# Scores as three float16 products with scaled queries and keys, from the eighteenth tile on, in an attention and channel-mix kernel

## The chip, the cores and the metric

The kernel runs on one core of a Trainium2 chip. The metric is the device time of one launch in microseconds. A core has five engines that each work through their own list of instructions in order: PE multiplies matrices (PEld, its weight load, overlaps it), DVE and POOL do elementwise work and reductions, ACT evaluates functions and scaled copies, and SP issues the DMA transfers. The engines wait for one another through semaphores.

## The reference

An attention without heads over pooled keys is followed by a channel mix. B is 4, there are N = 12288 queries of C = 128 channels per batch, and the keys and values are the same 768 vectors per batch.

```python
kv_pool = kv.reshape(B, H // r, r, W // r, r, C).mean(axis=(2, 4))     # r = 4
k = v = kv_pool.reshape(B, -1, C) @ w_sr                               # 768 x 128
s = (q @ k.transpose(0, 2, 1)) / sqrt(C)
a = exp(s - s.max(-1)); a /= a.sum(-1) + 1e-09
x = a @ v
xk = mu_k * x + (1.0 - mu_k) * x_prev        # x_prev: the row before, zero at the start
xr = mu_r * x + (1.0 - mu_r) * x_prev
kk = np.maximum(xk @ w_k, 0.0)               # 128 -> 1024
out = sigmoid(xr @ w_r) * (kk * kk @ w_v)    # 1024 -> 128
```

The inputs make the scores and the gates large, so every product of matrices is carried to more than one half-precision factor.

## The kernel before

The work is cut into tiles of 512 queries, 24 per batch; the last one is cut in two of 256, so there are 97 tiles. One tile goes through these steps. Their short names are the keys of the tables that set the order.

- `qf` loads the queries (channels on partitions), `qh` (ACT) rounds them to float32r, `ql` (POOL) is the rest in bfloat16.
- `S0` to `S3` (PE): scores of 128 queries against 768 keys, in a PSUM buffer of two banks. Each is three products in two chunks of columns (256 and 512): `ql` with the keys in bfloat16, the upper half of `qh` read as bfloat16 with the rest of the keys (`kbl` holds both), and `qh` with the keys in float32r (`ksh`).
- `nm` (DVE): the row maximum, negated. `ex` (ACT): exponential with `nm` as bias and the row sum as a second output. `rc` (DVE): the reciprocal of the sums. `f1` (ACT) and `f2` (DVE): the weights in float16 and their rest. `tt` (SP): the DMA transposes into `pT`.
- `AV0` to `AV5` (PE): 18 products of 512 columns into `px`. `xe`, `xc`, `x`, `xh`, `xl` on ACT, POOL and DVE: the mix with the row before, split in two float16 halves.
- `ha`, `hb` 0 to 3 (PE): the first layer, two blocks of 128 each, 24 products. `r`, `k2`, `kh`, `kl`: relu and square on ACT and DVE, the split on ACT, DVE and POOL. `va`, `vb` (PE): the second layer, 24 products. `z` (PE): the gate, 3 products; `th`, `E`, `T1`, `E1`, `g` finish it; `o` multiplies, `so` stores.

Each group of instructions is added to a plan with a number as its time: the entry of its name in a table plus the tile's place times PERIOD (19.3). All groups of all tiles are issued in the order of these numbers, and each engine gets its instructions in that order. The tables are ONCE (weights and first batch), EARLY (the first 8 tiles), WHEN (the tiles between), LATE (the last 5), PREP and SUM (the keys of the next batch). SUM adds one load and one reduction of 64 keys (`L`, `br`) to each of 12 tiles of each of the first three batches; PREP adds the projection (`pk`), scale statistics (`am` to `xt`, `sv`) and the splits of the keys (`ksh`, `kb`, `kd`, and `vh`, `vl`, `tv` for the values).

PSUM holds three buffers of two banks in a ring named "big", which the four scores and the four blocks of the first layer of each tile take in turn, and one bank each named "x" (`px`, `pz`, and the small products of the preparation) and "v" (`pv`). A product can be issued only once the buffer's last user has been read. Three of the four exponentials are written to SBUF; that of `S3` stays in PSUM until `f2`. Of the four blocks of the first layer, `k2` of block 3 is written over the product in PSUM, and DVE makes its `kl` from there.

In the profile nearly all instructions carry line 39, the helper that records them. So groups are told apart by the tiles that they write and read.

Of the kernel before, what the change touches and what calls it, by code (L numbers as in the profile page):

```python
# [73 lines left out]
def tile_kernel(ctx, tc, qT, kv0a, kv0b, kvw, head, w_k, w_v, w_r, outT):  # L74
# [16 lines left out]
    scale = 1.0 / math.sqrt(C)  # L91

# [26 lines left out]
    for name, shape, dtype in (  # L119
# [11 lines left out]
        ("ks", [P, K], F32), ("acc", [P, K], F32), ("dg", [P, 2, P], BF16), ("di", [P, P], F32),  # L131
# [319 lines left out]
    def batch_prep(b, i0, res):  # L451
# [18 lines left out]
        ex, exs, ivs = (one(n) for n in ("ex", "exs", "ivs"))  # L470
        xt, xi = (one(n, n=2) for n in ("xt", "xi"))
        exi = one("exi", I32)

        for n, (c0, c1) in enumerate(CHUNKS):
            @at(f"ksh{n}")
            def _(n=n, c0=c0, c1=c1):
                if later:
                    dve.tensor_copy(out=put("ksh")[:, c0:c1], in_=ks[:, c0:c1])
                else:
                    act.activation(  # L480
                        out=put("ksh")[:, c0:c1], in_=pks[n][:, 0:c1 - c0], func=AF.Copy,
                        scale=scale / WIN,
                    )

            @at(f"kb{n}")
            def _(n=n, c0=c0, c1=c1):
                if later:
                    pool.tensor_copy(out=put("kbl")[:, 0, c0:c1], in_=ks[:, c0:c1])
                else:
                    act.activation(  # L490
                        out=put("kbl")[:, 0, c0:c1], in_=pks[n][:, 0:c1 - c0], func=AF.Copy,
                        scale=scale / WIN,
                    )

            @at(f"kd{n}")
            def _(n=n, c0=c0, c1=c1):
                if later:
                    pool.tensor_tensor(
                        out=put("kbl")[:, 1, c0:c1], in0=ks[:, c0:c1],
                        in1=res["ksh"][:, c0:c1].bitcast(F32), op=ALU.subtract,  # L500
                    )
                else:
                    dve.scalar_tensor_tensor(
                        out=put("kbl")[:, 1, c0:c1], in0=pks[n][:, 0:c1 - c0], scalar=scale / WIN,
                        in1=res["ksh"][:, c0:c1].bitcast(F32), op0=ALU.mult, op1=ALU.subtract,
                    )
# [74 lines left out]
    def plan_tile(i, b, t0, T, at0):  # L581
# [36 lines left out]

        @at("qh")
        def _():  # L620
            act.copy(out=new("qh"), in_=st["qf"])

        @at("ql")
        def _():
            pool.tensor_tensor(
                out=new("ql"), in0=st["qf"], in1=st["qh"].bitcast(F32), op=ALU.subtract
            )

        for s in range(NSUB):
# [18 lines left out]

            @at(f"ex{s}")
            def _(s=s):  # L650
# [4 lines left out]
                else:  # L655
# [3 lines left out]
                    bias=st[f"nm{s}"], scale=1.0, accum_out=st[f"sm{group[s]}"][:, s:s + 1],  # L659
# [238 lines left out]
    bps = {b: {} for b in range(B)}  # L898

# [19 lines left out]
BUFS = {'pe': 4, 'nm': 4, 'sm': 4, 'rc': 4, 'pp': 4, 'kk': 3, 'kh': 4, 'kl': 4, 'kv': 6, 'rr': 2, 'ks': 1, 'acc': 1, 'dg': 1, 'vv': 1, 'di': 2}  # L919
FIRST = [512]  # L920
LAST = [256, 256]
ENGINE = {'wq': 'P', 'wp': 'P', 'wd': 'P', 'cz': 'P', 'cv': 'P', 'uz': 'P', 'vl': 'P', 'am': 'D'}
BLOCKS = [2, 2, 2, 2, 2, 2, 2, 2]
GROUP = 8

WHEN = {
# [7 lines left out]
    "xck": 141.87398, "xek": 142.03537, "xer": 142.22498, "xk": 142.40427, "xr": 142.58396,  # L934
# [19 lines left out]
    "L": 65.37223, "br": 79.195,  # L954
# [339 lines left out]
```

## Time and profile before

| what | value |
|---|---|
| median of 3 runs | 1876.15 us (1875.62 to 1876.49) |
| profiled execution, its own time | 1878.05 us |
| its span in the trace | 1876.3 us |
| PE, PEld busy | 1842.5 us (98%), 932.4 us (50%) |
| DVE, ACT, POOL busy | 1711.5 us (91%), 1698.2 us (91%), 1061.1 us (57%) |
| mean granted clock of PE | 0.996 |
| DMA queue of SP, share of 16 engines | 59.6%, 230.43 MB |

Busy time is the time in which at least one instruction of the engine runs. Two instructions of an engine that follow each other overlap at their ends, so busy times of single instructions add up to more than the engine's. The ends of products on PE are modelled; their starts are not, so the distance from one start to the next is the better measure there.

### The profile page before, as it was taken

The page shows a single profiled execution, that of the slowest core. Times are in us where ns is not written, and L with a number is a line of the kernel's source. Part 1 is how long each engine was busy: PE and PEld are TensorE (multiplying, and loading weights), DVE is VectorE, ACT ScalarE, POOL GpSimd, SP SyncE. Part 2 cuts the span into 40 slices and gives each one's busy share as a digit, 9 for nine tenths or more (in the row PEclk, how much of TensorE's full clock was granted, in tenths as well). Part 3 has the DMA queues.
Part 4 walks back from the last instruction along what each step waited for, and adds up shares of the span by engine and source line. Part 5 has one row for each costly group of instructions (what it writes and reads, how often), then busy time and mean ns, then how long its engine had stood idle before and what let it go on. Part 6 is the DMA issues. An engine that isn't in the chain of part 4 may idle for free.

```text
span 1876.3 us, 26840 instructions
## 1 busy us (share of the span) xinstructions
PE 1842.5 (98%) x8918; PEld 932.4 (50%) x9065; DVE 1711.5 (91%) x2383; ACT 1698.2 (91%) x2454; POOL 1061.1 (57%) x818
## 2 busy tenths in 40 slices
PE   6999999999999999999999999999999999999999
PEld 3444455454545455555555454545455555555545
DVE  6899999999899999999989999999998989898898
ACT  5998999999999999999999999989999999999987
POOL 3555655565555555556555565656555555555556
PEclk8999999999999999999999999999999999999999
DMA  7766566565657675656555666747465556555462
GB/s 230 141 136 143 124 151 117 112 122 108 117 124 146 135 144 138 115 110 119 113 112 129 146 134 143 139 101 131 102 119 107 115 110 116 110 111 109 92 118 61
DMA packets 644235, 232.15 MB, mean 124 GB/s; under 512 B 612352, under 2 KB 613120, under 8 KB 644096
## 3 DMA queue, kind: packets, MB, share of 16 engines
q1 hardware_dynamic: 644096, 230.43, 59.6%
q8 instruction: 71, 1.16, 0.3%
q14 instruction: 68, 0.56, 0.1%
HBM read 52.63 MB, written 25.17 MB: 41 GB/s over the span
## 4 chain that ended last, share of the span: by engine, by line
PE 91%; DVE 1%; issue 1%; DMA 0%; ACT 0%; SPq 0%; DVEq 0%; ACTq 0%
PE ph L39 25%; PE pv L39 25%; PE px L39 19%; PE S L39 19%; PE pz L39 4%; DMA pT<-pp 0%; PE pk L39 0%; DVE pp L39 0%; DVE nm L39 0%; DVE kk L39 0%; DVE xr L39 0%; ACT kh L39 0%; DVE xk L39 0%; ACT xer L39 0%; DVE kl L39 0%
## 5 line engine op out<-in xcount | busy, mean ns | idle before, releaser
L39 POOL TENSOR_TENSOR kl<-kk,kh 128x1024 bf16<-128x1024 f32 (+1 forms) x291 | 663.7, 2281 | 238.1 <-ACT kh L39 186.1
L39 ACT ACTIVATE rr<-ph 128x1024 f32<-128x1024 f32 (+1 forms) x388 | 393.2, 1015 | 59.0 <-PE ph L39 46.6
L39 DVE TENSOR_REDUCE nm<-S 128x1 f32<-128x768 f32 x384 | 364.9, 952 | 69.8 <-PE S L39 69.5
L39 PE MATMUL px<-pT,vT 128*128 128x512 f16 (+1 forms) x1746 | 393.1, 378 | 0.9 <-DMA pT<-pp 0.6
L39 ACT ACTIVATE kh<-rr 128x1024 f16<-128x1024 f32 (+1 forms) x291 | 305.0, 1049 | 1.3 <-PE pv L39 0.8
L39 DVE SCALAR_TENSOR_TENSOR pp<-pe,rc,pp 128x768 f16<-128x768 f32 x289 | 293.6, 1018 | 2.6 <-ACT pp L39 2.4
L39 PE MATMUL pv<-kh,wvl 128*128 128x512 f16 (+1 forms) x776 | 294.7, 381 | 0.0
L39 PE MATMUL ph<-xkh,wkl 128*128 128x512 f16 (+1 forms) x776 | 292.2, 377 | 0.7 <-ACT pe L39 0.3
L39 PE MATMUL ph<-xkh,wkh 128*128 128x512 f16 (+1 forms) x776 | 292.2, 377 | 0.0
L39 PE MATMUL pv<-kh,wvh 128*128 128x512 f16 (+1 forms) x776 | 292.1, 377 | 0.0
L39 PEld LDWEIGHTS <-vT 128*128 128x128 f16 x1746 | 170.4, 98 | 205.3 <-issue 2.4
L39 PE MATMUL S<-ksh,qh 128*128 128x512 f32 (+1 forms) x768 | 270.7, 434 | 0.0
L39 ACT ACTIVATE pp<-pe,rc 128x768 f16<-128x768 f32 x289 | 267.9, 931 | 1.0 <-DMA pT<-pp 0.9
L39 ACT ACTIVATE pe<-S,nm 128x768 f32<-128x768 f32 x289 | 260.1, 900 | 6.8 <-DVE nm L39 6.6
L39 POOL TENSOR_TENSOR xrl<-xr,xrh 128x512 f16<-128x512 f32 (+1 forms) x97 | 112.1, 1155 | 271.9 <-DVE xrh L39 271.9
L39 PE MATMUL S<-kbl,qh 128*128 128x256 bf16 (+1 forms) x768 | 252.7, 329 | 3.0 <-issue 0.2
L39 POOL TENSOR_TENSOR xkl<-xk,xkh 128x512 f16<-128x512 f32 (+1 forms) x97 | 114.7, 1182 | 243.7 <-DVE xkh L39 237.5
L39 DVE TENSOR_TENSOR kk<-ph,rr 128x1024 f32<-128x1024 f32 (+1 forms) x194 | 233.9, 1206 | 15.9 <-ACT rr L39 15.9
L39 PEld LDWEIGHTS <-wkh 128*128 128x128 f16 x1552 | 151.4, 98 | 179.4 <-issue 2.8
L39 PE MATMUL ph<-xkl,wkh 128*128 128x512 f16 (+1 forms) x776 | 228.8, 377 | 0.1
L39 PE MATMUL S<-kbl,ql 128*128 128x512 bf16 (+1 forms) x714 | 215.0, 326 | 5.8 <-DVE pp L39 3.0
L39 PE MATMUL pv<-kl,wvb 128*128 128x512 bf16 (+1 forms) x683 | 201.1, 377 | 2.6
(118 smaller groups left out, 2628.2 us busy)
## 6 DMA issues: line engine op xcount, KB each, us to landing
qf<-qT SPq DMA_DIRECT2D x95, 256.0 KB, 3.0
outT<-o SPq DMA_DIRECT2D x95, 256.0 KB, 3.3
kvt<-kvw SPq DMA_DIRECT2D x36, 512.0 KB, 4.7
pT<-pp SPq DMA_TRANSPOSE x384, 3.9
kva<-kv0a SPq DMA_DIRECT2D x8, 512.0 KB, 8.2
kvb<-kv0b SPq DMA_DIRECT2D x4, 512.0 KB, 5.8
land<-moe_w_k SPq DMA_DIRECT2D x2, 512.0 KB, 6.1
land<-moe_w_v SPq DMA_DIRECT2D x2, 512.0 KB, 7.3
```

Of the source, the lines that this page charges most:

```text
L39: return self.tc.keep_in_program_order(op(*args, **kwargs))
```

## The change

Tiles 0 to 16 keep the scores described above. From tile 17 on (`half`), the queries of eight tiles (a turn; `GROUP`) share one scale, and the keys of a batch another:

- `Lq` loads a tile's queries a second time, nine tiles ahead (`AHEAD`), and `mq` (ACT) takes the sum of their absolute values per channel, with an accumulated output. At the last tile of a turn, `qr` (DVE) takes the largest of the eight, `qd` (ACT) puts it on a diagonal, `qb` (PE) multiplies by ones so that every partition has all 128 values, `qt` (DVE) takes the largest, and `qg` (DVE) makes the scale and its inverse. The sum bounds the largest value from above.
- `qs` (POOL) multiplies the loaded queries by the inverse scale in place; `qh` and `ql` are float16 then.
- A third diagonal block (`dg`, `dm`, `xt` have three columns now) gives the largest key of a batch; `kfh` (ACT) and `kfl` (DVE) make the keys' two float16 parts in `kf`. They take the place of `ksh`, `kb` and `kd` for the second to fourth batch, whose keys no longer have them; the first batch has both.
- `S` is `ql` with the upper keys, `qh` with the lower, `qh` with the upper, all float16.
- `gs` (DVE) is the product of the two scales per turn and batch; `nm` is followed by a multiplication by it (DVE, one column), and `ex` has it as its scale operand.

The numbers of all tables are new as well, so the order of the whole program differs. PERIOD, the ring sizes (but for one of the new tiles) and the split of the other work over the engines are the same. WHEN has 93 entries where it had 84.

```diff
+    AHEAD = GROUP + 1
+    half_from = START
...
-        for n, (c0, c1) in enumerate(CHUNKS):
+        for n, (c0, c1) in enumerate(CHUNKS if not later else []):
             @at(f"ksh{n}")
...
+            dve.tensor_scalar_mul(st["dg"][:, 2, :], ident, ex)
...
         @at("sv")
         def _():
             dve.reciprocal(xi, xt)
+            dve.tensor_scalar_mul(sk, xi[:, 2:3], X_TOP)
+            dve.tensor_copy(out=put("bk"), in_=xt[:, 2:3])
...
+        @at("kfh")
+        def _():
+            act.activation(out=put("kf")[:, 0, :], in_=ks, func=AF.Copy, scale=sk)
+
+        @at("kfl")
+        def _():
+            dve.scalar_tensor_tensor(
+                out=put("kf")[:, 1, :], in0=ks, scalar=sk, in1=put("kf")[:, 0, :],
+                op0=ALU.mult, op1=ALU.subtract,
+            )
...
+        half = i >= half_from
+        turn, place = divmod(i - half_from, GROUP)
+
+        if half_from <= i + AHEAD < NTILES:
+            b2, t2, T2, _at2 = seq[i + AHEAD]
+            turn2, place2 = divmod(i + AHEAD - half_from, GROUP)
+            ends = place2 == GROUP - 1 or i + AHEAD == NTILES - 1
+            gq = groups.setdefault(turn2, {})
+
+            @at("Lq")
+            def _():
+                st["qm"] = take("qm")
+                sp.dma_start(out=st["qm"][:, 0:T2], in_=qT[b2, :, t2:t2 + T2])
+
+            @at("mq")
+            def _():
...
+                if ENGINE["mq"] == "A":
+                    act.activation(
+                        out=take("ju")[:, 0:T2], in_=st["qm"][:, 0:T2], func=AF.Abs,
+                        accum_out=gq["mq"][:, place2:place2 + 1],
+                    )
...
+            if ends:
+                @at("qr")
+                def _():
+                    dve.tensor_reduce(
+                        out=one("qr"), in_=gq["mq"][:, 0:place2 + 1], axis=AX.X, op=ALU.max
+                    )
+
+                @at("qd")
+                def _():
+                    gq["dq"] = take("dq")
+                    act.activation(out=gq["dq"], in_=ident, func=AF.Copy, scale=one("qr"))
+
+                @at("qb")
+                def _():
+                    gq["pq"] = take("x", name="pq")[:, 0:P]
+                    pe.matmul(gq["pq"], lhsT=ones, rhs=gq["dq"], start=True, stop=True)
+
+                @at("qt")
+                def _():
+                    dve.tensor_reduce(out=one("qt"), in_=gq["pq"], axis=AX.X, op=ALU.max)
+
+                @at("qg")
+                def _():
+                    gq["bq"], gq["sq"] = take("bq"), take("sq")
+                    dve.tensor_scalar(
+                        gq["bq"], one("qt"), 2.0 ** -90, 1.0 / X_TOP, op0=ALU.max, op1=ALU.mult
+                    )
+                    dve.reciprocal(gq["sq"], gq["bq"])
...
+        if half:
+            @at("qs")
+            def _():
+                eng("qs").tensor_scalar_mul(st["qf"], st["qf"], groups[turn]["sq"])
...
+                if half:
+                    kf = bps[b]["kf"]
+                    for c0, c1 in CHUNKS[::-1]:
+                        for m, (w, h) in enumerate(((ql, 0), (qh, 1), (qh, 0))):
+                            pe.matmul(
+                                S[:, c0:c1], lhsT=w, rhs=kf[:, h, c0:c1], start=(m == 0), stop=(m == 2)
+                            )
+                    return
...
+                if half:
+                    st["gs"] = units[turn, b]
+                    dve.tensor_scalar_mul(st[f"nm{s}"], st[f"nm{s}"], st["gs"])
...
-                    bias=st[f"nm{s}"], scale=1.0, accum_out=st[f"sm{group[s]}"][:, s:s + 1],
+                    bias=st[f"nm{s}"], scale=st["gs"] if half else 1.0, accum_out=st[f"sm{group[s]}"][:, s:s + 1],
...
+START = 17
...
-    "qf": 58.22684, "qh": 90.77762, "ql": 96.17481, "S0": 103.60711, "S1": 103.79064,
+    "qf": 59.2816, "Lq": 60, "mq": 80, "qs": 86, "qh": 90.45951, "qr": 93.6, "ql": 93.65377,
+    "qd": 93.8, "qb": 94.2, "qt": 94.6, "qg": 95, "S0": 105.76747, "S1": 106.49731,
```

The first place is PE at one score in the middle of the program. Names ahead of the arrow are what is written, names behind it what is read. Before, it is:

```order
L39 LDWEIGHTS ql
L39 MATMUL S<-kbl,ql 128x256
L39 LDWEIGHTS qh
L39 MATMUL S<-kbl,qh 128x256
L39 LDWEIGHTS ql
L39 MATMUL S<-kbl,ql 128x512
L39 LDWEIGHTS qh
L39 MATMUL S<-kbl,qh 128x512
L39 MATMUL S<-ksh,qh 128x512
L39 MATMUL S<-ksh,qh 128x256
```

Now the same place reads:

```order
L39 LDWEIGHTS ql
L39 MATMUL S<-kf,ql 128x256
L39 LDWEIGHTS qh
L39 MATMUL S<-kf,qh 128x256
L39 LDWEIGHTS qh
L39 MATMUL S<-kf,qh 128x256
L39 LDWEIGHTS ql
L39 MATMUL S<-kf,ql 128x512
L39 LDWEIGHTS qh
L39 MATMUL S<-kf,qh 128x512
L39 LDWEIGHTS qh
L39 MATMUL S<-kf,qh 128x512
```

The two float32r products, whose weight loads are not instructions of their own here, are gone, and all six products have a weight load of the same kind.

The second place is DVE between the last two row maxima of a tile and the next block of the gate. Before:

```order
L39 TENSOR_TENSOR ph<-ph,rr 128x1024
L39 TENSOR_REDUCE nm<-S 128x1
L39 TENSOR_TENSOR kl<-ph,kh 128x1024
L39 TENSOR_REDUCE nm<-S 128x1
L39 TENSOR_SCALAR E<-E,sc 128x512
L39 TENSOR_SCALAR th<-th 128x512
L39 SCALAR_TENSOR_TENSOR E<-th,E 128x512
L39 TENSOR_SCALAR rc<-sm 128x4
L39 RECIPROCAL rc<-rc 128x4
```

Now, in a tile that ends a turn of eight:

```order
L39 TENSOR_TENSOR ph<-ph,rr 128x1024
L39 TENSOR_REDUCE nm<-S 128x1
L39 TENSOR_SCALAR nm<-nm,gs 128x1
L39 TENSOR_TENSOR kl<-ph,kh 128x1024
L39 TENSOR_REDUCE nm<-S 128x1
L39 TENSOR_SCALAR nm<-nm,gs 128x1
L39 TENSOR_REDUCE qr<-mq 128x1
L39 TENSOR_REDUCE qt<-pq 128x1
L39 TENSOR_SCALAR bq<-qt 128x1
L39 RECIPROCAL sq<-bq 128x1
L39 TENSOR_SCALAR E<-E,sc 128x512
L39 TENSOR_SCALAR th<-th 128x512
```

Each row maximum has its multiplication right behind it, and in one tile of eight the four small instructions of the turn stand ahead of the gate and of `rc`.

The third place is ACT from the gate of one tile to the first relu of the next. Before:

```order
L39 ACTIVATE E<-pz,uz 128x512
L39 ACTIVATE th<-pz,uz 128x512
L39 ACTIVATE pe,sm<-S,nm 128x768
L39 ACTIVATE S,sm<-S,nm 128x768
L39 ACTIVATE rr<-ph 128x1024
```

Now, in a tile that ends a turn:

```order
L39 CAST qh<-qf 128x512
L39 ACTIVATE th<-pz,uz 128x512
L39 ACTIVATE E<-pz,uz 128x512
L39 ACTIVATE pe,sm<-S,nm,gs 128x768
L39 ACTIVATE dq<-ident,qr 128x128
L39 ACTIVATE S,sm<-S,nm,gs 128x768
L39 ACTIVATE ju,mq<-qm 128x512
L39 ACTIVATE rr<-ph 128x1024
```

The exponentials read `gs` besides `nm`, the pass over the second copy of the queries stands between the last exponential and the first relu, and in one tile of eight `dq` stands between the two exponentials.

More of the change, by code (lines that the diff above doesn't have):

```diff
@@ L130, in tile_kernel @@
         ("s4", [P, 4], F32), ("uz", [P, 2], F32), ("sc", [P, 1], F32),
-        ("ks", [P, K], F32), ("acc", [P, K], F32), ("dg", [P, 2, P], BF16), ("di", [P, P], F32),
+        ("ks", [P, K], F32), ("acc", [P, K], F32), ("dg", [P, 3, P], BF16), ("di", [P, P], F32), ("kf", [P, 2, K], F16), ("qm", [P, T], F32), ("mq", [P, GROUP], F32), ("ju", [P, T], BF16),
+        ("bk", [P, 1], F32), ("bq", [P, 1], F32), ("sq", [P, 1], F32), ("gs", [P, 1], F32), ("dq", [P, P], BF16),
     ):
@@ L469, in batch_prep @@
         pks = later_keys(b, i0, at, ks) if later else first_keys(ks)
-        ex, exs, ivs = (one(n) for n in ("ex", "exs", "ivs"))
-        xt, xi = (one(n, n=2) for n in ("xt", "xi"))
+        ex, exs, ivs, sk = (one(n) for n in ("ex", "exs", "ivs", "sk"))
+        xt, xi = (one(n, n=3) for n in ("xt", "xi"))
         exi = one("exi", I32)
-        for n, (c0, c1) in enumerate(CHUNKS):
+        for n, (c0, c1) in enumerate(CHUNKS if not later else []):
             @at(f"ksh{n}")
             def _(n=n, c0=c0, c1=c1):
[L477 to L483, printed above, removed]
+                act.activation(
+                    out=put("ksh")[:, c0:c1], in_=pks[n][:, 0:c1 - c0], func=AF.Copy, scale=scale / WIN
+                )
@@ L485, in _ @@
             @at(f"kb{n}")
             def _(n=n, c0=c0, c1=c1):
[L487 to L493, printed above, removed]
+                act.activation(
+                    out=put("kbl")[:, 0, c0:c1], in_=pks[n][:, 0:c1 - c0], func=AF.Copy,
+                    scale=scale / WIN,
+                )
@@ L495, in _ @@
             @at(f"kd{n}")
             def _(n=n, c0=c0, c1=c1):
[L497 to L506, printed above, removed]
+                dve.scalar_tensor_tensor(
+                    out=put("kbl")[:, 1, c0:c1], in0=pks[n][:, 0:c1 - c0], scalar=scale / WIN,
+                    in1=res["ksh"][:, c0:c1].bitcast(F32), op0=ALU.mult, op1=ALU.subtract,
+                )
@@ L556, in _ @@
                 )
+            dve.tensor_scalar_mul(st["dg"][:, 2, :], ident, ex)
         @at("dm")
         def _():
-            st["dm"] = take("x", name="dm", shape=[P, 2, P])
+            st["dm"] = take("x", name="dm", shape=[P, 3, P])
             pe.matmul(st["dm"], lhsT=ones, rhs=st["dg"], start=True, stop=True)
@@ L574, in _ @@
                 )
+        @at("kfh")
[3 more added lines that the diff above has]
+        def _():
+            dve.scalar_tensor_tensor(
+                out=put("kf")[:, 1, :], in0=ks, scalar=sk, in1=put("kf")[:, 0, :],
+                op0=ALU.mult, op1=ALU.subtract,
+            )
         @at("uz")
@@ L617, in _ @@
             sp.dma_start(out=new("qf"), in_=qT[b, :, t0:t0 + T])
+        half = i >= half_from
[11 more added lines that the diff above has]
+            def _():
+                if "mq" not in gq:
+                    gq["mq"] = take("mq")
+                if ENGINE["mq"] == "A":
+                    act.activation(
+                        out=take("ju")[:, 0:T2], in_=st["qm"][:, 0:T2], func=AF.Abs,
+                        accum_out=gq["mq"][:, place2:place2 + 1],
+                    )
+                else:
+                    dve.tensor_reduce(
+                        out=gq["mq"][:, place2:place2 + 1], in_=st["qm"][:, 0:T2], axis=AX.X,
+                        op=ALU.max, apply_absolute_value=True,
+                    )
+            if ends:
+                @at("qr")
+                def _():
+                    dve.tensor_reduce(
+                        out=one("qr"), in_=gq["mq"][:, 0:place2 + 1], axis=AX.X, op=ALU.max
+                    )
+                @at("qd")
[14 more added lines that the diff above has]
+                        gq["bq"], one("qt"), 2.0 ** -90, 1.0 / X_TOP, op0=ALU.max, op1=ALU.mult
+                    )
+                    dve.reciprocal(gq["sq"], gq["bq"])
@@ L619, in _ @@
+        if half and (place == 0 or t0 == 0 or i == half_from):
+            @at("gs")
+            def _():
+                units[turn, b] = take("gs")
+                dve.tensor_scalar(
+                    units[turn, b], groups[turn]["bq"], bps[b]["bk"], 1.0 / X_TOP, op0=ALU.mult,
+                    op1=ALU.mult,
+                )
+        if half:
+            @at("qs")
+            def _():
+                eng("qs").tensor_scalar_mul(st["qf"], st["qf"], groups[turn]["sq"])
         @at("qh")
@@ L620, in _ @@
         def _():
-            act.copy(out=new("qh"), in_=st["qf"])
+            if half:
+                st["qh"] = take("qh", shape=[P, TOP], dtype=F16)[:, 0:T]
+            else:
+                new("qh")
+            act.copy(out=st["qh"], in_=st["qf"])
         @at("ql")
         def _():
+            if half:
+                st["ql"] = take("ql", dtype=F16)[:, 0:T]
+            else:
+                new("ql")
             pool.tensor_tensor(
-                out=new("ql"), in0=st["qf"], in1=st["qh"].bitcast(F32), op=ALU.subtract
+                out=st["ql"], in0=st["qf"], in1=st["qh"] if half else st["qh"].bitcast(F32),
+                op=ALU.subtract,
@@ L631, in _ @@
             def _(s=s):
-                ksh, kbl = bps[b]["ksh"], bps[b]["kbl"]
                 S = st[f"S{s}"] = take("big", name="S")
@@ L635, in _ @@
                 qh, ql = st["qh"][:, sl], st["ql"][:, sl]
+                if half:
+                    kf = bps[b]["kf"]
[3 more added lines that the diff above has]
+                                S[:, c0:c1], lhsT=w, rhs=kf[:, h, c0:c1], start=(m == 0), stop=(m == 2)
+                            )
+                    return
+                ksh, kbl = bps[b]["ksh"], bps[b]["kbl"]
                 qb = st["qh"].bitcast(BF16).rearrange("p (t h) -> p t h", h=2)[:, sl, 1]
@@ L647, in _ @@
                 )
+                if half:
+                    st["gs"] = units[turn, b]
+                    dve.tensor_scalar_mul(st[f"nm{s}"], st[f"nm{s}"], st["gs"])
             @at(f"ex{s}")
@@ L898, in tile_kernel @@
     bps = {b: {} for b in range(B)}
+    groups, units = {}, {}
     batch_prep(0, 0, bps[0])
@@ L918 @@
 PAIRS = 8
-BUFS = {'pe': 4, 'nm': 4, 'sm': 4, 'rc': 4, 'pp': 4, 'kk': 3, 'kh': 4, 'kl': 4, 'kv': 6, 'rr': 2, 'ks': 1, 'acc': 1, 'dg': 1, 'vv': 1, 'di': 2}
+BUFS = {'pe': 4, 'nm': 4, 'sm': 4, 'rc': 4, 'pp': 4, 'kk': 3, 'kh': 4, 'kl': 4, 'kv': 6, 'rr': 2, 'ks': 1, 'acc': 1, 'dg': 1, 'vv': 1, 'di': 2, 'ju': 1}
 FIRST = [512]
 LAST = [256, 256]
-ENGINE = {'wq': 'P', 'wp': 'P', 'wd': 'P', 'cz': 'P', 'cv': 'P', 'uz': 'P', 'vl': 'P', 'am': 'D'}
+ENGINE = {'wq': 'P', 'wp': 'P', 'wd': 'P', 'cz': 'P', 'cv': 'P', 'uz': 'P', 'vl': 'P', 'am': 'D', 'mq': 'A', 'qs': 'P'}
 BLOCKS = [2, 2, 2, 2, 2, 2, 2, 2]
 GROUP = 8
+START = 17
 WHEN = {
[7 rows of a table removed]
-    "xck": 141.87398, "xek": 142.03537, "xer": 142.22498, "xk": 142.40427, "xr": 142.58396,
[9 rows of a table removed]
[8 rows of a table added]
+    "AV2": 143.76038, "xcr": 144.20781, "xek": 144.74705, "xer": 145.91357, "xk": 146.12634,
[9 rows of a table added]
 }
 PREP = {
[4 rows of a table removed]
[3 rows of a table added]
 }
 SUM = {
-    "L": 65.37223, "br": 79.195,
+    "L": 60.34821, "br": 75.22001,
 }
 ONCE = {
[30 rows of a table removed]
[28 rows of a table added]
+    "kfl": 213.51421,
 }
@@ L1146 @@
     {
[17 rows of a table removed]
-    },
-    {
[7 rows of a table removed]
-        "xck": 142.94987, "xek": 144.24683, "xk": 145.03802, "xer": 145.9814, "xr": 146.10995,
[9 rows of a table removed]
-    },
-    {
[7 rows of a table removed]
-        "AV4": 142.50543, "xek": 143.55947, "xk": 144.17765, "xkh": 144.80629, "xer": 146.00366,
[9 rows of a table removed]
-    },
-    {
[5 rows of a table removed]
-        "xek": 138.09887, "xk": 142.47605, "xr": 142.53025, "xkh": 143.84478, "xkl": 147.51737,
[9 rows of a table removed]
-    },
-    {
[5 rows of a table removed]
-        "xck": 148.36922, "xk": 148.39723, "xr": 149.91817, "xkh": 150.7783, "xkl": 152.61305,
[9 rows of a table removed]
[7 rows of a table added]
+        "xcr": 142.18496, "xck": 142.18855, "xer": 143.40538, "xek": 143.56156, "xr": 143.85997,
+        "xk": 144.31728, "xkh": 151.18973, "xrh": 152.30643, "xkl": 154.54183, "ha0": 154.67368,
[8 rows of a table added]
+    },
+    {
[7 rows of a table added]
+        "AV1": 141.58135, "xcr": 142.34413, "xek": 143.8, "xer": 145.993, "xk": 146.17206,
[9 rows of a table added]
+    },
+    {
[17 rows of a table added]
+    },
+    {
[5 rows of a table added]
+        "xek": 142.20235, "xk": 142.37284, "xkh": 144.92548, "xkl": 145.19568, "xer": 145.25123,
[9 rows of a table added]
+    },
+    {
[5 rows of a table added]
+        "xer": 154.07119, "xek": 154.27859, "xr": 154.34528, "xrh": 155.56082, "xrl": 157.34039,
[9 rows of a table added]
     },
```

11 lines of the change are left out of this document (3 added, 8 removed), and 509 rows, old and new, of tables (EARLY, LATE, ONCE, PREP).

## The prediction

> **What bounds the kernel now.** I read the page's busy shares and its chain of waits first, then the chain in order of time, then PE's instructions around one score, then the busy time by stretch, and last the groups of instructions of ACT, DVE and POOL.
>
> ```profile
> span 1876.3 us, 26840 instructions
> PE 1842.5 (98%) x8918; PEld 932.4 (50%) x9065; DVE 1711.5 (91%) x2383; ACT 1698.2 (91%) x2454; POOL 1061.1 (57%) x818
> PE 91%; DVE 1%; issue 1%; DMA 0%; ACT 0%; SPq 0%; DVEq 0%; ACTq 0%
> ```
>
> PE alone makes up 91% of the chain. In order of time (start, length, what), the chain shows the same piece again and again, the 18 products of `px`:
>
> ```profile
> 749.32 3.88 PE px L39 x18
> 769.79 3.88 PE px L39 x18
> ...
> 978.26 3.88 PE px L39 x18
> 997.20 3.88 PE px L39 x18
> 1016.14 3.88 PE px L39 x18
> ```
>
> From one to the next are 18.94 us, to the hundredth, tile after tile. Where the keys of a batch are prepared it is 20.47 once (749.32 to 769.79), for PE has its own products to add there. One product of 512 columns takes 3.88 / 18 = 0.2156 us. A tile has 18 + 24 + 24 + 3 = 69 of them outside the scores, 14.87 us. The four scores get the rest, 18.94 - 14.87 = 4.07 us, or 1.017 each. So the tile is PE's list without gaps, and only what shortens this list, or puts a gap in it, moves the time.
>
> PE's instructions around one score (start, length, engine, operation):
>
> ```profile
> 1010.65 0.27 PE L39 MATMUL S<-kbl,ql 128*128 128x256 bf16 x1
> 1010.75 0.27 PE L39 MATMUL S<-kbl,qh 128*128 128x256 bf16 x1
> 1010.86 0.38 PE L39 MATMUL S<-kbl,ql 128*128 128x512 bf16 x1
> 1011.08 0.38 PE L39 MATMUL S<-kbl,qh 128*128 128x512 bf16 x1
> 1011.11 0.70 PE L39 MATMUL S<-ksh,qh 128*128 128x512 f32 x2
> 1011.65 0.39 PE L39 MATMUL pv<-kh,wvl 128*128 128x512 f16 x1
> ```
>
> By the starts a score takes 1.00 us up to the next product; the tile's sum gives 1.017, the difference being a slower first product behind it.
>
> **The change part by part.** *The products.* The number of columns stays the same: three times 768. The float32r pair was already nearly as fast as half precision, so this is not a change from slow to fast products. The trace has chains of 256-column float16 products with a weight load each, in the last tile:
>
> ```profile
> 1859.74 0.27 PE L39 MATMUL ph<-xkh,wkh 128*128 128x256 f16 x1
> 1859.84 0.27 PE L39 MATMUL ph<-xkh,wkl 128*128 128x256 f16 x1
> 1859.95 0.27 PE L39 MATMUL ph<-xkh,wkh 128*128 128x256 f16 x1
> 1860.06 0.38 PE L39 MATMUL ph<-xkl,wkh 128*128 128x256 f16 x2
> ```
>
> Their starts are 0.32 / 3 = 0.107 apart. A float16 score is then 3 x (0.2156 + 0.107) = 0.968 us. Against 1.00 it saves 0.03, against 1.017 it saves 0.049; four scores save 0.12 to 0.20 us per tile. The tile's sum is measured end to end, so I lean to its side and take 0.165. Tiles 17 to 96 are 78 whole and two half ones, 79 in all: 13.0 us (bounds 9.5 to 15.8). A tile then has 18.94 - 0.165 = 18.775 us for every other engine.
>
> *ACT and DVE must fit into that.* Busy time in one tile without and one with a reduction of the next batch's keys, and at both ends of the program (start:end, length, then each engine):
>
> ```profile
> core 0: us, PE busy (x) PEld busy (x) DVE busy (x) ACT busy (x) POOL busy (x), PEclk, DMA share, GB/s
> 420.00:438.94 18.94, 18.89 (x94) 9.51 (x93) 17.03 (x27) 17.42 (x26) 10.31 (x9) 1.00 0.57 99
> 610.00:628.94 18.94, 18.89 (x94) 9.53 (x94) 17.97 (x25) 17.42 (x26) 11.02 (x9) 1.00 0.65 139
> ...
> 0.00:52.00 52.00, 33.23 (x110) 17.40 (x113) 36.50 (x82) 28.63 (x53) 20.05 (x26) 0.89 0.75 229
> ...
> 1793.00:1876.30 83.30, 77.63 (x432) 43.36 (x436) 72.01 (x103) 67.83 (x99) 50.69 (x41) 1.00 0.37 78
> ```
>
> Groups of ACT (busy us, mean ns, then its idle time just before and who ended it):
>
> ```profile
> L39 ACT ACTIVATE rr<-ph 128x1024 f32<-128x1024 f32 x380 | 388.5, 1024 | 57.6 <-PE ph L39 46.6 <-ACT xer L39 0.3 <-ACT kh L39 0.3
> L39 ACT ACTIVATE kh<-rr 128x1024 f16<-128x1024 f32 x285 | 301.3, 1058 | 0.7 <-PE pv L39 0.5
> L39 ACT ACTIVATE S<-S,nm 128x768 f32<-128x768 f32 x95 | 83.1, 875 | 72.4 <-DVE nm L39 72.1
> L39 ACT ACTIVATE E<-pz,uz 128x512 f32<-128x512 f32 x95 | 65.3, 687 | 0.0
> L39 ACT ACTIVATION_READ_ACCUMULATOR pe<-S,nm 128x1 f32 x289 | 59.8, 207 | 0.0
> L39 ACT CAST qh<-qf 128x512 fp32r<-128x512 f32 x95 | 58.1, 611 | 6.5 <-DMA qf<-qT 6.5
> ```
>
> `mq` is a pass over 512 columns without a pointer operand, like `qh`, and a read of the accumulator: 0.611 + 0.207 = 0.82 us. The scale of the exponentials becomes a pointer. `E` has one and takes 687 ns, `qh` has none and takes 611; four exponentials gain between 0 and 4 x 0.076 = 0.30 us. ACT goes from 17.42 to 18.24 or at most 18.54 us per tile, 97 to 99% of 18.775. It has 1.52 us idle now and 0.24 to 0.54 then. What fills that idle time now are waits: 72.4 / 95 = 0.76 us for `nm` and 57.6 / 95 = 0.61 us for the first layer.
>
> Groups of DVE:
>
> ```profile
> L39 DVE SCALAR_TENSOR_TENSOR pp<-pe,rc,pp 128x768 f16<-128x768 f32 x289 | 293.6, 1018 | 2.6 <-ACT pp L39 2.4
> L39 DVE TENSOR_TENSOR ph<-ph,rr 128x1024 f32<-128x1024 f32 x95 | 116.8, 1229 | 3.3 <-ACT rr L39 0.2
> L39 DVE TENSOR_TENSOR kl<-ph,kh 128x1024 bf16<-128x1024 f32 x95 | 115.4, 1215 | 2.2 <-ACT kh L39 1.1 <-DVE ph L39 0.5
> L39 DVE SCALAR_TENSOR_TENSOR pp<-S,rc,pp 128x768 f16<-128x768 f32 x95 | 96.0, 1010 | 1.3 <-ACT pp L39 1.1
> L39 DVE TENSOR_SCALAR sc<-cv,xt 128x1 f32<-128x1 f32 x3 | 0.8, 268 | 0.0
> L39 DVE TENSOR_SCALAR exi<-ex 128x1 int32<-128x1 int32 x4 | 0.6, 154 | 0.1
> ```
>
> The multiplication behind each `nm` depends on it and has one column: between `exi` (154 ns, a constant operand) and `sc` (268, pointers), 0.62 to 1.07 us for four. DVE goes from 17.03 to 17.65 to 18.10 us, and in the 24 tiles after the 17th that reduce keys from 17.97 to 18.59 to 19.04. All but the upper end of the last fits.
>
> *Do the waits stay?* I take it that they shrink. A wait shows that an engine was early; an engine that is 0.5 us later finds its data there. What matters is how late it may be before PE lacks a buffer. The tightest is the one that block 3 of the first layer leaves. In the new order PE issues 28 products' worth between that block and the first block of the next tile, which takes the buffer: `vb` 2, `va` 4, score 4.5, gate 3, `vb` 2, score 4.5, `va` 8, or 28 x 0.2156 = 6.0 us. In that time `rr`, `kh`, `ph` and `kl` must be through: 1.024 + 1.058 + 1.229 + 1.215 = 4.5 us in a row. So 1.5 us of lateness cost nothing, more than ACT's extra 0.82 to 1.12 us. I cost `mq`, the pointer and the row multiplications at nothing, covered by PE's list; without that cover each 0.1 us of a tile is 7.9 us.
>
> *The turn's scale, ten times.* `pq` has 128 columns, under half of 0.107 to 0.107 us of PE. On DVE, `qt` must wait for PE to come to `pq`, behind a block of the first layer, and `E`, `T1`, `rc` and the next tile's `f1` queue behind it; this uses up the 1.5 us. I take 0.3 us for each turn in all (0 to 1): 3 us.
>
> *POOL and DMA.* `qs` is one pass of 512 columns, between the cast and the two-operand subtraction here, so 0.61 to 1.28 us:
>
> ```profile
> L39 POOL TENSOR_TENSOR ql<-qf,qh 128x512 bf16<-128x512 f32 x95 | 121.7, 1281 | 11.0 <-ACT qh L39 11.0
> L39 POOL CAST kbl<-ks 128x512 bf16<-128x512 f32 x3 | 1.8, 614 | 0.0
> ```
>
> POOL is busy 11.02 of 18.94 us, so it fits. SP gets one more issue per tile, queued ahead of three of the four transposes; the transfers are at 0.57 to 0.65 of their time. Nothing, 0 to 2 us. *Preparation:* two passes of 768 columns for `kf` replace `ksh` on DVE and work on POOL: 1 us (0 to 3).
>
> *The new order at both ends.* PE idles 18.8 us of the first 52 and 5.7 of the last 83. The first block of keys and the last store are unavoidable. In the new order the product for the weights' scales stands ahead of the second chunk of keys and of all scores. That puts the maximum over the weights into the way of the first score; other work of ACT moves forward in return. I take 1 us of loss, bounds 6 either way.
>
> **The sum** on the span: 1876.3 - 13.0 + 3 + 1 + 1 = 1868.3. The median lies 0.15 below the span (the profiled execution's own time of 1878.05 is 1.9 above the median), so 1868.
>
> **The rivals.** *ACT sets the pace.* For it: 97 to 99%, and in-order waits of 0.76 and 0.61 us that an order must hide. Against it: the 1.5 us of buffer. If the wait for `nm` stays, a tile is 18.24 + 0.76 = 19.00 us at least and 18.54 + 0.76 = 19.30 at most, 0.06 to 0.36 above 18.94: 5 to 28 us more over 79 tiles, and 5 for the other terms, 1886 to 1909. It decides from 0.40 us of remaining waits on.
>
> *DVE sets the pace in the 24 tiles that reduce keys.* The other 55 gain 9.1. At 19.04 the 24 lose 0.1 each, and 5 for the rest: 1875. If the 0.97 us that DVE idles there stay, 18.59 + 0.97 = 19.56 us, 14.9 lost: 1887. Nearly full, it would be pushed over by anything that slows it, `qs` above all: held for its 0.61 to 1.28 us, DVE would need 19.2 to 20.3 in these tiles, 6 to 33 lost, 1878 to 1905. The Trainium skill has such a rule: the page "SBUF — State Buffer", section "SBUF: two separate sides", says that POOL and a DVE instruction with two inputs in SBUF lock each other out for a whole instruction. The trace does not bear it out on DVE's side: `pp<-pe` with both inputs in SBUF takes 1018 ns and `pp<-S` with one in PSUM 1010, with POOL busy 57% of the time. So I give that little.
>
> *The change doesn't do what it says:* six weight loads cost what the float32r pair cost; then the other terms remain, 1881. The 0.107 us of the last tile speak against it. *The new order is simply better at the start:* 6 us better instead of 1 worse, 1861.
>
> **How the numbers follow.** My forecast has 0.66 and on its own 1862 to 1873. ACT's pace has 0.12, DVE's 0.11, no saving 0.05, a better start 0.06. The range 1859 to 1880 leaves out the slow ends of ACT and DVE and a little below. A measurement of this kernel tells 0.2%, 3.8 us, from no change. Faster than 1872.4: most of 0.66, the 0.06 and a little of DVE's case, 0.70. Within: 0.12, from the edge of the forecast and DVE's mild end. Slower: 0.18.
>
> **What would show it.** Right: `px` to `px` at 18.75 to 18.82 us from tile 19 on, a score at 0.97, PE at 98% still, ACT and DVE at 95% or more with shorter waits. Wrong: gaps on PE in front of scores or first-layer blocks, released by ACT or DVE, in all tiles (ACT) or in the 24 with reductions (DVE); `px` to `px` unequal in tiles that end a turn by more than 1 us; or a first `px` much later than 52 us.

## The result: 4.5% slower, and the profile after

The changed kernel takes 1960.85 us (median of 5 runs, 1959.46 to 1963.59) where the kernel before takes 1876.49 (1875.62 to 1877.93). The ratio is 1.0452, with a 95% interval of 1.0436 to 1.0467. Forecast were 1868 us, and 1859 to 1880 as the range.

The page of the changed kernel begins so (span; busy time of each engine, its share, and its instructions):

```profile
span 1959.1 us, 27431 instructions
PE 1864.8 (95%) x8969; PEld 889.8 (45%) x9075; DVE 1799.7 (92%) x2762; ACT 1769.2 (90%) x2628; POOL 1208.1 (62%) x886
```

No engine is full: PE has fallen from 98% to 95%, and neither ACT nor DVE has come above 92%. What sets the time then? First where it is lost. The starts of the first products of `px`, as PE's timeline shows them, at tile 17, in the steady part, and in the last tiles:

```profile
370.07 3.19 PE L39 MATMUL px<-pT,vT 128*128 128x512 f16 x14
...
1460.21 4.05 PE L39 MATMUL px<-pT,vT 128*128 128x512 f16 x18
1480.23 4.05 PE L39 MATMUL px<-pT,vT 128*128 128x512 f16 x18
1500.25 4.05 PE L39 MATMUL px<-pT,vT 128*128 128x512 f16 x18
...
1761.66 1.67 PE L39 MATMUL px<-pT,vT 128*128 128x512 f16 x7
1781.07 2.11 PE L39 MATMUL px<-pT,vT 128*128 128x512 f16 x9
...
1839.44 1.89 PE L39 MATMUL px<-pT,vT 128*128 128x512 f16 x8
```

The same two tiles, 17 and 90, in the kernel before:

```profile
370.36 2.97 PE L39 MATMUL px<-pT,vT 128*128 128x512 f16 x13
...
1756.29 1.89 PE L39 MATMUL px<-pT,vT 128*128 128x512 f16 x8
```

Between tile 17 and tile 90 lie 1469.37 us now and 1385.93 before: 83.4 us, all of the 82.8 by which the span grew. Up to tile 17, and from tile 90 to the end, the program takes 0.3 to 0.4 us less than before. Most tiles take 20.02 us where they took 18.94. That is 1.08 us in each of 73 tiles, 79 of the 83.4 us; the rest lies in tiles at the end of a turn and where keys are prepared, which grew a little more. Two things are odd about the 20.02. They hold in tiles with and without a reduction of keys alike (671.85 to 691.87 is a tile with one), so it is not DVE's load. And near the end, where no `mq` is left to do, a tile takes 19.41 (1761.66 to 1781.07), exactly 0.61 less.

The saving in the products is there. PE around the third score of a tile (start, length; the idle time of PE and who ended it in brackets):

```profile
1490.60 0.38 PE L39 MATMUL pv<-kh,wvh 128*128 128x512 f16 x1
1491.88 0.27 PE L39 MATMUL S<-kf,ql 128*128 128x256 f16 x1 [0.90 <-ACT pe L39]
...
1492.85 0.38 PE L39 MATMUL pz<-xrh,wrl 128*128 128x512 f16 x1
```

A score takes 1492.85 - 1491.88 = 0.97 us. But PE stands still for 0.90 us ahead of it, waiting for ACT to read the buffer, and such waits stand in 77 places. The view of the waits says who waits for whom (total us, times, longest):

```profile
ACT pe L39 <- DVE nm L39: 98.1, 87, 2.5
DVE xk L39 <- ACT xer L39: 87.5, 79, 1.6
PE S L39 <- ACT pe L39: 58.3, 77, 1.6
ACT S L39 <- DVE nm L39: 42.6, 66, 1.4
```

PE waits for ACT, ACT for DVE, and DVE for ACT. Two of these waits close a ring, and it can be followed for one tile. ACT, from the last exponential of one tile (written over `S` in PSUM) to that of the next:

```profile
1477.94 0.96 ACT L39 ACTIVATE S<-S,nm,gs 128x768 f32<-128x768 f32 x1 [0.65 <-DVE nm L39]
...
1478.93 0.61 ACT L39 ACTIVATE ju<-qm 128x512 bf16<-128x512 f32 x1
1479.45 0.19 ACT L39 ACTIVATION_READ_ACCUMULATOR ju<-qm 128x1 f32 x1
1479.54 1.01 ACT L39 ACTIVATE rr<-ph 128x1024 f32<-128x1024 f32 x1
...
1485.56 0.69 ACT L39 ACTIVATE xek<-px,s 128x512 f32<-128x512 f32 x1
1486.12 1.06 ACT L39 ACTIVATE kh<-rr 128x1024 f16<-128x1024 f32 x1
1487.07 1.03 ACT L39 ACTIVATE rr<-ph 128x1024 f32<-128x1024 f32 x1
1487.98 0.70 ACT L39 ACTIVATE xer<-px,s 128x512 f32<-128x512 f32 x1
...
1490.74 0.99 ACT L39 ACTIVATE pe<-S,nm,gs 128x768 f32<-128x768 f32 x1 [1.12 <-DVE nm L39]
...
1497.96 0.96 ACT L39 ACTIVATE S<-S,nm,gs 128x768 f32<-128x768 f32 x1 [0.65 <-DVE nm L39]
```

DVE, over the second half of the same time:

```profile
1488.78 0.75 DVE L39 SCALAR_TENSOR_TENSOR xk<-px,s,xek 128x512 f32<-128x512 f32 x1 [1.43 <-ACT xer L39]
1489.45 0.95 DVE L39 TENSOR_REDUCE nm<-S 128x1 f32<-128x768 f32 x1
1490.43 0.21 DVE L39 TENSOR_SCALAR nm<-nm,gs 128x1 f32<-128x1 f32 x1
1490.57 0.95 DVE L39 TENSOR_REDUCE nm<-S 128x1 f32<-128x768 f32 x1
...
1496.65 0.95 DVE L39 TENSOR_REDUCE nm<-S 128x1 f32<-128x768 f32 x1
1497.63 0.21 DVE L39 TENSOR_SCALAR nm<-nm,gs 128x1 f32<-128x1 f32 x1
```

ACT works without a gap from 1477.94 to the end of `xer` at 1488.68: 10.74 us. 0.10 later DVE starts `xk`, which had waited 1.43 for `xer`, and works without a gap to the end of the last multiplication of `nm` at 1497.84: 9.06 us. 0.12 later ACT starts the last exponential, which had waited for that. 10.74 + 0.10 + 9.06 + 0.12 = 20.02. The work is handed back and forth once per tile, so no tile can be shorter than this ring, although each engine in it has idle time at another place of its list.

What the change put into the ring can be read off. The step for `mq` on ACT is 1478.93 to 1479.54, 0.61. From one maximum of `nm` to the next are now 1490.57 - 1489.45 = 1.12 us with the multiplication between them. In the kernel before DVE goes on 643.27 - 642.41 = 0.86 after a maximum:

```profile
642.41 0.95 DVE L39 TENSOR_REDUCE nm<-S 128x1 f32<-128x768 f32 x1
643.27 1.01 DVE L39 SCALAR_TENSOR_TENSOR pp<-pe,rc,pp 128x768 f16<-128x768 f32 x1
```

So a multiplication adds about 0.25, and the four of them 1.0. Last, the pointer on the last exponential adds 0.09 (963 ns against 876). Without them the ring would be 20.02 - 0.61 - 1.0 - 0.09 = 18.3 us, hidden behind PE's 18.94. The place of `xer` is the other part of it. In the kernel before, ACT did `xer` right behind `xek`:

```profile
639.71 0.69 ACT L39 ACTIVATE xek<-px,s 128x512 f32<-128x512 f32 x1
640.28 0.70 ACT L39 ACTIVATE xer<-px,s 128x512 f32<-128x512 f32 x1
640.90 1.02 ACT L39 ACTIVATE rr<-ph 128x1024 f32<-128x1024 f32 x1
```

Now `kh` and `rr` stand between, 1487.98 - 1486.12 = 1.86 us more. But `xk` reads `px` and `xek`, not `xer`. Why it waits for it is the first question for the experiments; whether the ring is the cause at all is the second.

### The profile page after: what moved, and what is told of

Same layout as the page of the kernel before. It is cut to its first block, busy times and chain, and to the rows that moved or that the text cites. A ratio compares the mean times of both kernels' runs of the same rounds, so it can differ in the third digit from the quotient of the medians.

```text
span 1959.1 us, 27431 instructions
## 1 busy us (share of the span) xinstructions
PE 1864.8 (95%) x8969; PEld 889.8 (45%) x9075; DVE 1799.7 (92%) x2762; ACT 1769.2 (90%) x2628; POOL 1208.1 (62%) x886
## 5 line engine op out<-in xcount | busy, mean ns | idle before, releaser
L39 POOL TENSOR_TENSOR kl<-kk,kh 128x1024 bf16<-128x1024 f32 (+1 forms) x291 | 640.8, 2203 | 193.7 <-ACT kh L39 158.2
L39 ACT ACTIVATE pe<-S,nm,gs 128x768 f32<-128x768 f32 x238 | 237.5, 998 | 91.6 <-DVE nm L39 91.6
L39 DVE SCALAR_TENSOR_TENSOR pp<-pe,rc,pp 128x768 f16<-128x768 f32 x289 | 316.9, 1117 | 2.3 <-ACT pp L39 2.0
L39 POOL TENSOR_TENSOR xkl<-xk,xkh 128x512 f16<-128x512 f32 (+1 forms) x97 | 144.6, 1491 | 273.5 <-DVE xkh L39 271.8
L39 PE MATMUL S<-kf,qh 128*128 128x256 f16 x1264 | 308.4, 326 | 0.0
L39 POOL TENSOR_TENSOR xrl<-xr,xrh 128x512 f16<-128x512 f32 (+1 forms) x97 | 146.8, 1514 | 224.0 <-DVE xrh L39 223.3
L39 ACT ACTIVATE pp<-pe,rc 128x768 f16<-128x768 f32 x289 | 260.3, 937 | 1.4 <-DVE rc L39 1.3
L39 PE MATMUL S<-kf,ql 128*128 128x256 f16 x632 | 205.6, 325 | 58.3 <-ACT pe L39 58.2
L39 PEld LDWEIGHTS <-qh 128*128 128x128 f16 (+1 forms) x1400 | 137.2, 98 | 163.2 <-issue 83.8
L39 PE MATMUL pv<-kl,wvb 128*128 128x512 bf16 (+1 forms) x680 | 195.0, 376 | 0.5
```

The source lines that it names most:

```text
L39: return self.tc.keep_in_program_order(op(*args, **kwargs))
```

## The experiments

All edits are to the changed kernel, most to the table WHEN; its numbers set only the order of issue. The theory is the ring. The rivals are that ACT is simply too full, that DVE is too full, and that the new order as a whole is worse.

**`xer` back behind `xek`.**

```diff
-    "xek": 144.74705, "xer": 145.91357, "xk": 146.12634,
+    "xek": 144.74705, "xer": 144.74805, "xk": 146.12634,
```

> One number of the table WHEN is changed: ACT's second copy of px (xer) is issued right behind the first (xek), as in the kernel before, where in the changed kernel a square (kh1) and a relu (rr2) stand between them. All work is the same. Loop theory: in the changed kernel ACT from the last exponential to xer (10.74 us) and DVE from xk to the last scaled row maximum (9.06 us) follow each other, with two handoffs of 0.11 us, which is the 20.02 us of its tiles. Without kh1 (0.95) and rr2 (0.90) in it the loop is 18.17 us, below the 18.78 us of PE's list; px to px is 18.8 us, 79 times 1.24 = 98 us are won, about 1863 us (1858 to 1880). Load theory: ACT and DVE have too much to do, wherever it stands; the same work stays at 1950 to 1965 us.

Measured: 1876.75 us, ratio to the kernel before 0.9999 (0.999 to 1.0009). This one number gives back 84 us with no instruction added or taken away. Tiles without reductions take 18.79 us, the pace of PE's shorter list; so ACT's load is not the bound. The exceptions are more than the ring theory had said: the first three of a batch's twelve tiles with reductions are nearly at that pace, but most of the others take 19.02 to 19.28, and so do one or two tiles behind each turn's end.

**`mq` out of the ring, `xer` left late.**

```diff
-    "qf": 59.2816, "Lq": 60, "mq": 80, "qs": 86,
+    "qf": 59.2816, "Lq": 60, "mq": 71.1, "qs": 86,
```

> One other number of WHEN is changed: ACT's pass for the queries' scale (mq) moves from behind the last exponential, inside the loop, to between the last square of a tile (kh3) and the rounding of the queries (qh), outside it. All work is the same; xer stays late. Loop theory: the loop loses 0.61 us, 19.41 us per tile as in the last tiles of the changed kernel, which have no mq; about 70 tiles, 1961 - 43 = 1918 us (1910 to 1930). Load theory: no change, 1955 to 1965 us.

Measured: 1973.56 us, 1.0516 (1.0495 to 1.0537), slower still. Most tiles without reductions take 19.41 us, just the 0.61 less that were expected; but nearly all tiles with reductions take 20.9 to 21.3, and one tile behind each turn's end takes 20.9, where the ring theory had no such step. In these tiles DVE (first two lines) and POOL (last line) show why:

```profile
661.93 1.00 DVE L39 SCALAR_TENSOR_TENSOR pp<-pe,rc,pp 128x768 f16<-128x768 f32 x1
...
662.99 2.77 DVE L39 SCALAR_TENSOR_TENSOR pp<-pe,rc,pp 128x768 f16<-128x768 f32 x1
```

```profile
662.81 2.13 POOL L39 TENSOR_TENSOR kl<-kk,kh 128x1024 bf16<-128x1024 f32 x1 [1.17 <-ACT kh L39]
```

The same instruction takes 1.00 and 2.77 us. The second began 0.18 us after POOL's `kl` and ended 0.82 us after it: it stood still until `kl` was through, with `xk` and the whole ring behind it. So the lock between DVE and POOL, which the prediction had set aside, counts here. In a tile without a reduction DVE is earlier; there the second `pp` starts 0.18 us ahead of `kl`, takes 1.00 us, and it is `kl` that grows, to 2.81 us.

**Both moves.** The two edits above together.

> Both moves. Loop theory: the loop is 17.56 us, 1.2 us below PE's list, which sets the pace with 18.78 us; within 5 us of the run with xer alone, about 1863 us, and less than it if there the turns or the batches' preparation still cost. Load theory: 1950 to 1965 us.

Measured: 1874.08 us, 0.9987 (0.9977 to 0.9996). Tiles without reductions take 18.79, and tiles with them mostly 19.04 (the first three of a batch's twelve still 18.79 to 18.85). In the slower ones DVE is busy 18.86 of 19.04 us (start:end, length, then the busy time of PE, PEld, DVE, ACT and POOL, PE's granted clock, and the share and GB/s of DMA):

```profile
651.09:670.13 19.04, 18.96 (x95) 8.96 (x93) 18.86 (x30) 18.48 (x28) 12.64 (x9) 1.00 0.66 154
```

With the ring gone DVE, nearly without a gap, looks like the bound there. Its list contains one instruction that is too long, and POOL's list shows `qs` (written in place, `qf<-qf,sq`) beside it:

```profile
652.79 1.44 DVE L39 SCALAR_TENSOR_TENSOR pp<-pe,rc,pp 128x768 f16<-128x768 f32 x1
654.15 1.00 DVE L39 SCALAR_TENSOR_TENSOR pp<-S,rc,pp 128x768 f16<-128x768 f32 x1
```

```profile
652.73 1.56 POOL L39 TENSOR_SCALAR qf<-qf,sq 128x512 f32<-128x512 f32 x1
```

From 420 us on, 69 of the 226 `pp<-pe` lie beside a `qs` and are 0.43 us longer on average. That raised the next question, whether moving `qs` alone takes this away (below).

**The new order with the old scores.** START is set beyond the last tile, the old keys `ksh`, `kb` and `kd` are made again with their old numbers, and `kfh`, `kfl` are left out; all other numbers are those of the change.

```diff
-START = 17
+START = 1000
...
-        for n, (c0, c1) in enumerate(CHUNKS if not later else []):
+        for n, (c0, c1) in enumerate(CHUNKS):
```

> The new order with the old scores: all tiles keep float32r and bfloat16 products, there is no second load of the queries, no turn's scale, no scaled row maximum; the keys of the second to fourth batch get ksh, kb and kd at the places that they had in the old table. Loop theory: the loop loses mq (0.61), four scaled maxima (0.66) and a pointer (0.09), 18.66 us, below PE's 18.94 with the old scores: 1870 to 1890 us. Rival, the new order alone is at fault (its start, its end or its buffers): above 1900 us.

Measured: 1876.91 us, 0.9999 (0.9989 to 1.001), with tiles of 18.93 to 18.96. The order, with its late `xer`, costs nothing by itself. The ring is there already, but by the sum above it has 18.3 us, less than PE's list; a wait that it leaves is visible, 107.2 us of idle time ahead of `xk` (40.0 before), and harmless:

```profile
L39 DVE SCALAR_TENSOR_TENSOR xk<-px,s,xek 128x512 f32<-128x512 f32 x95 | 71.2, 750 | 107.2 <-ACT xer L39 106.4 <-ACT xek L39 0.8
```

So it takes both: the order with its late `xer` is not slow without the new steps, and the new steps are not slow with `xer` early.

**`xk` ahead of `xer` in the program.** The lists of ACT and POOL stay as in the changed kernel, `xer` late; only DVE's `xk` is put into the plan before it.

```diff
-    "xer": 145.91357, "xk": 146.12634,
+    "xer": 145.91357, "xk": 145.9,
```

> From the changed kernel, with xer late as there: one number of WHEN is changed so that DVE's xk is given to the plan just before ACT's xer, no longer behind it. The lists of ACT and POOL stay the same, DVE's nearly so; what changes is that xk, which reads only px and xek, no longer stands behind another engine's earlier read of px. Loop theory: xk waits for xer only because xer comes ahead of it in the program; then it starts behind xek and DVE's own work, 1.4 us earlier, the loop is 18.6 us or less and PE sets the pace: 18.8 to 19.1 us per tile, 1870 to 1885 us, close to the run with xer moved. Rival: xk needs POOL's copy into xek or another transfer that comes late, or ACT's and DVE's load sets 20.02; then 1950 to 1965.

Measured: 1888.92 us, 1.0065 (1.0051 to 1.0079). Tiles without reductions take 18.79: the ring is open although `xer` is as late as before. `xer` and `xk` share only `px` and the constants in `s`, and both only read them. So the wait comes from the order in which the program names two readers of one tile on two engines, the later waiting for the earlier; that the tile is `px` in PSUM, and not `s`, is likely but not shown. With the order reversed the wait is reversed too, and this line of the waits, 0.8 us in the changed kernel, has grown:

```profile
ACT xer L39 <- DVE xk L39: 39.3, 47, 2.8
```

The time is a little above what was expected, because in six tiles `pp` is again held by `kl` (two of them take 3.88 us in one), with `xer` now waiting behind. Three lie behind a turn's end and take 21.1 to 21.4, and the other three, tile 16 and two behind a preparation of keys, take 20.7 to 20.8. They are about 2 us each longer than in the run with only `xer` moved, which is nearly all of the 12 us between these two runs.

**`qs` elsewhere.** The kernel with both moves, and `qs` just ahead of `xkl`.

```diff
-    "mq": 71.1, "qs": 86,
+    "mq": 71.1, "qs": 71.4,
```

> From the run with both moves (xer behind xek, mq outside the loop): POOL's scaling of the queries (qs) moves from between xrl and xer, where it starts at the same time as DVE's pp<-pe of the first score, to just ahead of xkl, where POOL idles and DVE has row maxima to do. All work is the same. Lock theory: pp<-pe, with both inputs in SBUF, is held there by 0.43 us in each tile (1.44 against 1.01 us); DVE, which in the 24 tiles with a reduction of keys is busy without a gap for 19.04 us, falls to 18.6, and PE's 18.79 sets the pace there: 24 times 0.25 = 6 us, about 1868 us (1865 to 1871). Load theory (DVE is full there whatever POOL does): no change, 1873 to 1875.

Measured: 1865.03 us, 0.9936 (0.9922 to 0.995). Tiles take 18.79 with and without reductions, and 18.85 at a turn's end. The first `pp` is short again, DVE's list fits, and PE is the bound in all tiles (timeline of DVE, then the tile in the view by stretch):

```profile
650.63 1.01 DVE L39 SCALAR_TENSOR_TENSOR pp<-pe,rc,pp 128x768 f16<-128x768 f32 x1
```

```profile
649.39:668.19 18.80, 18.75 (x94) 9.11 (x94) 18.62 (x30) 18.57 (x29) 12.57 (x10) 1.00 0.68 155
```

The work on each engine is the same as with both moves. Only the time at which POOL does `qs` differs, and 9 us go.

**The turn's scale later on DVE.** The kernel before this one, with `qt` and `qg` behind the last maximum of the tile.

```diff
-    "qd": 93.8, "qb": 94.2, "qt": 94.6, "qg": 95,
+    "qd": 93.8, "qb": 94.2, "qt": 98.8, "qg": 98.9,
```

> The run before this one, and in the one tile of eight that ends a turn, DVE's qt, bq and sq come behind E and th, when pq is long there, no longer ahead of them. With the other order such a tile takes 0.25 us more than its neighbours and the one before it 0.06. If the wait for pq is what costs, up to 10 times 0.25 = 2.5 us less, 1865.5; if the small instructions themselves or PE's product cost it, no change.

Measured: 1863.58 us, 0.9932 (0.9919 to 0.9944), the fastest of all, and faster than both kernels. It is 1.45 us under the run before it, but the two sets of five executions overlap, and the profiled ones differ by 1.9 us, of which the edit explains only 0.7: the second tile of a turn's end went from 18.86 to 18.79 in seven places (the run before had taken most of its 0.25 away already), and two tiles of preparation from 20.19 to 20.08. Another 1.2 us lie in one tile near the end (17.80 to 16.59), behind the last turn, where the edit changes nothing. So that the edit made the kernel faster as a whole is not shown; at most some 0.7 us are its own. Its page:

```profile
span 1861.3 us, 27505 instructions
PE 1829.4 (98%) x8969; PEld 898.6 (48%) x9075; DVE 1773.2 (95%) x2762; ACT 1780.0 (96%) x2628; POOL 1192.2 (64%) x886
```

## Why the prediction was wrong

**The step that failed is "Do the waits stay? I take it that they shrink."** Its reason was "an engine that is 0.5 us later finds its data there". That holds for a chain that begins and ends at PE and has slack. It does not hold for a ring: there every engine that is later makes the next one later, and the first gets its own delay back a tile on. The prediction checked one buffer, that of block 3 of the first layer (6.0 against 4.5 us), and took it for the tightest. The ring of `xer`, `xk`, `nm` and the last exponential was not looked for. The profile of before had a sign of it, among the groups of DVE:

```profile
L39 DVE SCALAR_TENSOR_TENSOR xk<-px,s,xek 128x512 f32<-128x512 f32 x95 | 71.1, 748 | 40.0 <-ACT xer L39 38.3 <-ACT xek L39 1.7
```

Here `xk` waits for an instruction whose output it does not read, so the wait is one that the order of the program makes. The order of the changed program has `kh` and `rr` between `xek` and `xer`, and the prediction did not look at this place. What went into the ring it could have estimated from its own rows: 0.61 for `mq`, 0.62 to 1.07 for the multiplications, and about 2 for the `kh` and `rr` ahead of `xer`. Measured were 0.61, 1.0, 0.09 for the pointer, and 1.86 for the place of `xer`.

The sign that the prediction had set down for ACT's pace, gaps on PE ahead of the scores, ended by ACT, in all tiles, did come. A ring through ACT leaves the same sign; the run with only `xer` moved, with ACT's work unchanged, tells the two apart.

**"I cost `mq`, the pointer and the row multiplications at nothing, covered by PE's list; without that cover each 0.1 us of a tile is 7.9 us."** The second half was right. 1.08 us more per tile are 7.9 x 10.8 = 85 us by that price, 83.4 by the trace.

**The sizes of the other terms were near.** A score was put at 0.968 us and takes 0.97; a tile that PE sets was put at 18.775 and takes 18.79 in five experiments. `mq` was put at 0.82 busy and is 0.620 + 0.192 = 0.81. The multiplication of `nm` was bounded by 0.62 and 1.07 for four and is 1.0 by its steps. The pointer came out above its bound: 998 ns against 902, so 0.096 where 0.076 was the most.

```profile
L39 ACT ACTIVATE ju<-qm 128x512 bf16<-128x512 f32 x78 | 48.4, 620 | 0.0
L39 ACT ACTIVATE pe<-S,nm,gs 128x768 f32<-128x768 f32 x238 | 237.5, 998 | 91.6 <-DVE nm L39 91.6
L39 ACT ACTIVATE pe<-S,nm 128x768 f32<-128x768 f32 x51 | 46.0, 902 | 6.5 <-DVE nm L39 6.5
L39 DVE TENSOR_SCALAR nm<-nm,gs 128x1 f32<-128x1 f32 x316 | 67.7, 214 | 11.2
L39 POOL TENSOR_SCALAR qf<-qf,sq 128x512 f32<-128x512 f32 x78 | 121.8, 1562 | 0.0
```

**`qs` was mis-sized**: 0.61 to 1.28 us were given, from a cast of one input and a subtraction of two, and it takes 1.56.

**"So I give that little", on the shared port, was wrong.** The argument was that `pp<-pe` takes 1018 ns on average although POOL is busy 57% of the time. The average only says that the two seldom collide in that order of the lists; it says nothing on what a collision costs. The trace of before has such a collision, with `pp` at 2.94 us instead of 1.01, beside `kl` on POOL:

```profile
1818.87 2.94 DVE L39 SCALAR_TENSOR_TENSOR pp<-pe,rc,pp 128x768 f16<-128x768 f32 x1
1818.87 2.13 POOL L39 TENSOR_TENSOR kl<-kk,kh 128x1024 bf16<-128x1024 f32 x1
```

In the changed kernel the average is 1117, with `mq` moved 1367, with both moves and `qs` moved 1025. The Trainium skill's page "SBUF — State Buffer", section "SBUF: two separate sides", says that whichever of the two starts first has the port for its whole instruction. For `kl` the trace agrees (2.77 us for 1.00, until `kl` ended). For `qs` it agrees in part: `pp` was held for 0.43 us of the 1.56.

**The rivals.** DVE setting the pace in the tiles with reductions was real, but behind the ring: with both moves these tiles took 19.04, the upper end that was given, and the kernel 1874, beside the rival's 1875. By sizes alone DVE's list fits, as the kernel with `qs` moved shows; what pushed it over was the reason named second, `pp` held by `qs`, for 0.43 us and not for 0.61 to 1.28. ACT setting the pace did not happen: ACT is full to 18.57 of 18.80 us in that kernel, and PE still sets the pace. The turn's scale was put at 0.3 each and costs 0.06 in its tile and 0.25 in the next with both moves. At the start, 1 us of loss was put in; there is 0.3 of gain by tile 17, and 3.2 with the ring opened and `qs` moved.

With the ring opened and `qs` moved the sum comes close: 1868.0 was forecast and 1865.03 measured. From tile 17 to tile 90 that kernel gains 9.6 us on the kernel before, where the sum had 13.0 less 3 and 1, or 9.0, for all its tiles; most of the rest of the gain is the better start.

## What to carry to other kernels

Before a few tenths of a microsecond are costed at nothing on engines that are not the bound, look for rings: follow one instruction of each busy engine to the one that it waits for, and on, until the chain comes back to the same engine a tile later; the length of that ring, not the engine's busy share, is what the additions count against. An instruction that waits for another whose output it does not read can mark such a place; here one number in the order opened it, and gave 84 us. An average duration does not clear a shared resource; look at the longest single cases, and at which starts would be brought together by the new order.

## What was unexpected in the hardware's behaviour

- One multiplication of 128x512 float32 by a pointer on POOL takes 1562 ns, more than a subtraction of two operands that writes float16 (`ql`, 1159) and 2.5 times a cast (614).
- A DVE instruction of 1.00 us took 2.77 when it started 0.18 us after a subtraction of 1024 columns on POOL, and 1.44 when it started 0.06 us after the multiplication of 512 columns.
- Not settled: `xkl` on POOL takes 1.49 to 1.51 us in all kernels with the new order, that with the old scores included, where it took 1.19 before. It was not seen on the path, and no run was made for it.
